# Another word order for the steady part of a fused convolution and SwiGLU kernel, and a list of its own for the second pair

## The chip, the cores and the metric

The kernel runs on one core of a Trainium2 chip. The metric is the device time of one execution in microseconds (us), the median over the runs shown. A core has a matrix engine (TensorE, PE; its weight loads are listed apart as PEld), VectorE (DVE), ScalarE (ACT), GpSimd (POOL), and SyncE (SP), on whose queue nearly all DMAs of this kernel are issued, each queue strictly in program order.

## What is computed

```python
# x: (8, 4096, 192), weight: (8 heads, 7 taps)
w = softmax(weight)                                    # over the taps
y[b, s, h, :] = sum_k w[h, k] * x_pad[b, s + k, h, :]  # causal, 24 channels a head
# y as (32768, 192); w_gate, w_val: (192, 1536), w_out: (1536, 192)
xn = y / sqrt(mean(y * y) + 1e-6) * rms_g
g, val = xn @ w_gate, xn @ w_val
out = (silu(g) * val) @ w_out                          # float32
```

## The kernel before

The 32768 tokens are cut into 32 pairs (p = 0 to 31) of 1024 tokens, each two blocks of 512. Pair 0 runs in its own prologue, pair 1 in plain float32 products (word list PLAIN for TensorE, FIRST for the rest). Pairs 2 to 31 are alike and make up most of the time.

**Gate products.** A pair's projections onto gate and value columns use a Strassen-like scheme: sums of blocks of the tokens times sums of blocks of the weights, 68 products a pair (names such as P1.0, Q3.5, Ab.3: kind, then column group j = 0 to 5). One product (`product`, L910) is 6 matmuls: the tokens were split into three parts whose products add up to float32 accuracy, and each part runs as two matmuls of 64 rows side by side. Its weights come from a ring of 10 slots in SBUF. There are 48 weight pieces a pair; when a piece's last product is recorded, the load of a new one into its slot (L790) is put on SP's queue, where it waits for that product. Products accumulate in PSUM banks (j, a) to (j, d); PSUM holds four such double banks, and `open` takes the one that is free, first come, first served.

**Between the products.** For each j: `f1` (ScalarE) copies bank a into b, `f3` (ScalarE) copies c into an SBUF tile, `f4` and `f5` (VectorE, L981) add that tile and b into c and into a new bank d. `g` (ScalarE, L987) takes the silu of the gate half of a bank, `m` (VectorE, L994) multiplies it with the value half into an SBUF tile, and with that the bank is free. So a chain Ag, Vm stands behind the last product of every bank: for (3,a) the last product is Ea.3, then come Aga.3 and Vma.3.

**o-steps.** The projection onto w_out is again Strassen-like: seven forms o1 to o7 for six j, 42 steps of 6 matmuls with tiles of 128 by 32 (`step`, L937), into accumulators X, Y, Z. The first step of form 1 opens X. Their inputs are the m tiles and sums of them (`h1` to `h4`, L964, on VectorE or GpSimd). `c1`, `c2`, `s7` copy accumulators, `C22` and `C21` (L1011) add them, `T11` to `T22` (L952) transpose results, `st` stores them.

**Work ahead for the next pairs.** `cv0` to `cv6` are the seven taps of the convolution (VectorE, L445; cv0 on ScalarE), `sq`, `red`, `pow`, `bc`, `mul` the norm, `pl.0` to `pl.7` put the result away to DRAM, `ft.0` to `ft.5` fetch it back turned (L646; for i = 1 and 3 nothing is issued), `x1` to `x4` (L832) form sums of token blocks, and `n`, `l`, `d` (L675, L818, L820) split the tokens into three parts, `ld.0` to `ld.7` load x.

**The order.** It is written by hand as words, one list for each pair (ORDER for all from 2 on), and recorded in that order; every engine runs its own words as they stand. The first letter is the engine (V VectorE, G GpSimd, A ScalarE, S SP's queue), then the action and its index; `+` and `-` shift the pair (`+` the next, `++` the one after, `-` the one before). `p3` records the next 3 entries of the pair's TensorE order LINE, `p3-` 3 of the pair before. LINE thus fixes TensorE's own order, ORDER where the rest stands against it. A tile framework adds the waits. In FIRST and for pair 1, a `+` word that was already done is skipped when it comes again.

Before, LINE has all 68 products and then all 42 o-steps. ORDER takes 2 products of a pair, then the last 6 steps of the pair before, then 66 products and 36 steps.

Of the kernel before, what the change touches and what calls it, by code (L numbers as in the profile page):

```python
# [20 lines left out]
def kernel(  # L21
# [36 lines left out]
    PAIRS = B * NB  # L58
# [15 lines left out]
    )  # L74
    PLAIN = (
        "a0 b0 c0 d0 o1.0 a1 b1 c1 d1 o1.1 a2 b2 c2 d2 o1.2 a3 b3 c3 d3 o1.3 a4 b4 c4 d4 o1.4",
        "a5 b5 c5 d5",
    )
    ORDER = (
# [14 lines left out]
    )  # L94
    FIRST = (
# [14 lines left out]
    )  # L110
    LINE = (
# [7 lines left out]
    )  # L119

    cst = ctx.enter_context(tc.tile_pool(name="cst", bufs=1))
# [8 lines left out]
    x_sb = {}  # L130
# [4 lines left out]
    def queue(eng):  # L135
        return nc.scalar if eng == "A" else nc.sync
# [8 lines left out]
    def load_head(p, b, t0, h, eng="S"):  # L145

        t = x_sb[p]

        def get(dst, tb, h, dims, r):
            row = x[b, t0 + tb * TB + r - HALO, h * GS :]  # L150
            src = bass.AP(
                tensor=row.tensor, offset=row.offset, ap=[dims, [D, TB + HALO - r], [1, GS]]
            )
            queue(eng).dma_start(out=dst, in_=src)

        first = int(t0 == 0)
        if first and h == 0:
            queue(eng).dma_start(out=t[0:H, 0:HALO, :], in_=zeros)
            get(t[0:H, HALO:, :], 0, 0, [GS, H], HALO)
        get(t[first * H + h :: H], first, h, [TB * D, P // H - first], 0)  # L160

    def load_part(p, h, eng):

        if h == 0:
            x_sb[p] = xs.tile([P, TB + HALO, GS], F32, name="xh")
        load_head(p, p // NB, (p % NB) * PT, h, eng)

# [203 lines left out]
    def convert_in(u):  # L371

        t = raw.pop(("in", u))
        dst = wf[:, :, u * NF : (u + 1) * NF, :].rearrange("p k f n -> p k (f n)")
        step = P if u == 0 else NF * P
        parts = [slice(i, i + step) for i in range(0, NF * P, step)]
        return [
            convert(t[:, :, c, :], exp_i[:, :, c], mf_i[:, :, c], dst[:, :, c], rg_sb, u < 2)
            for c in parts
        ]  # L380
# [5 lines left out]
    scr = {}  # L386
# [405 lines left out]
    def ring_start():  # L792
        ring[0] = spc.tile([P, NSLOT, KP * P], F32, name="ring")
        for slot in range(NSLOT):
            ring_load(slot)
# [40 lines left out]
    class Pair:  # L836
        def __init__(self, p):
            self.p = p
            self.bk, self.o_sb, self.sg = {}, {}, {}
            self.open_half, self.turned = {}, [0, 0]  # L840
            self.line = self.products()

        def hv(self, j, c):
# [74 lines left out]
        def step(self, form, k):  # L918
            b = ACC[form]
            if form in (1, 7) and b not in self.bk:  # L920
                full4.discard(self.open(b, False))
            fresh = form in (1, 7) and k == 0
            src = hs[:, k, :] if form == 5 else self.hv(k, LEFT[form])
            right = RIGHT[form][:, HOME[k]]
            self.tiles(b, [right[:, m] for m in range(NM)], src, fresh)
# [122 lines left out]
        tap(p, k, eng)  # L1048

    def put_away(p, h, eng):  # L1050
        if h == 0:
            scr[p] = dram.tile([D, PT], F32, name="xd")
        to = scr[p][:].rearrange("(h a) (b t) -> h b a t", a=GS, t=TB)
        queue(eng).dma_start(out=to[h], in_=yn[p][h::H])

    def ahead(eng, name, p):

        act, *at = name.split(".")
        i = int(at[0]) if at else 0
        if act[0] == "x":  # L1060
            x_sum(int(act[1]), eng, p)
        elif act in ("n", "l", "d"):
            split(act, i, eng, p)
        elif act == "ft":
            fetch(p, i, eng)
        elif act == "pl":
            put_away(p, i, eng)
        elif act == "ld":
            load_part(p, i, eng)
        elif act[0:2] == "cv":  # L1070
            tap_of(p, int(act[2]), eng)
        else:
            {"sq": square, "red": reduce, "pow": factor, "bc": spread, "mul": scale}[act](p)
# [124 lines left out]
    p, sl, v = plain(first_hts)  # L1198
# [46 lines left out]
    def run(words, w):  # L1245
        for word in words:
            p = w + word.count("+") - word.count("-")
            if word[0] == "p":
                for _ in range(int(word[1:].rstrip("+-"))):
                    if p in pairs:  # L1250
                        next(pairs[p].line)
            elif word == "W":
                next(ready)()
            elif word == "R":
                ring_start()
            else:
                eng, name = word[0], word[1:].rstrip("+-")
                act = name.split(".")[0]
                if act in own_acts:
                    if own_acts[act] <= p < PAIRS and (name, p) not in ahead_done:  # L1260
                        ahead(eng, name, p)
                        if w == 1:
                            ahead_done.add((name, p))
                elif p in pairs:
                    pairs[p].do(eng, name)

    run([w for row in FIRST for w in row.split()], 1)
    for w in range(2, PAIRS + 1):
        run([w for row in ORDER for w in row.split()], w)
# [1 line left out]
_INS = ['x', 'weight', 'moe_w_gate', 'moe_w_val', 'moe_w_out', 'moe_rms_g']  # L1271
# [26 lines left out]
```

## Time and profile before

| | us |
|---|---|
| median of 3 runs (2474.97 to 2477.09) | 2475.02 |
| span of the profiled execution | 2476.6 |
| the slowest of the runs | 2477.09 |

The profile is of one execution of its own. In its views PE's pieces of work are given with start, length, engine, tile, line and count. The chain that ended last is followed back from the last instruction, at each step to what released it. In the waits, a line names who waited, who released it, the total in us, how often, and the longest. In a row with windows, after the length stand the busy times of PE, PEld, DVE, ACT and POOL with counts, then the granted clock, the DMA share and GB/s. A row of a timeline ends with the engine's idle time before it and what ended it.

### The profile page before, as it was taken

To read this page: it belongs to the slowest core of one execution; us is meant where nothing else is said; L and a number is where in the kernel's file an instruction comes from. 1 tells how busy PE (TensorE), PEld (TensorE's weight loads), DVE (VectorE), ACT (ScalarE), POOL (GpSimd) and SP (SyncE) were. 2 spreads that over 40 slices of the span, in tenths; PEclk is the share of its full clock that TensorE was granted. 3 is DMA by queue.
4 is the path that set the end of the run, shared out by engine and by line. 5 is a ranking of instruction groups with operands and counts; after the bars stand their busy time and mean duration, and the time that the engine had idled before them with its cause. 6 is when DMAs were issued, how large, how long until landed. Compare 5 with 4: busy or idle time off the path is not lost.

```text
span 2476.6 us, 69229 instructions
## 1 busy us (share of the span) xinstructions
PE 2454.1 (99%) x29152; PEld 1896.0 (77%) x29152; DVE 2020.8 (82%) x2526; ACT 1018.0 (41%) x1435; POOL 836.2 (34%) x624
## 2 busy tenths in 40 slices
PE   8999999999999999999999999999999999999999
PEld 5546777877777877777787778777777877778777
DVE  8687888888888888888888887888888888888864
ACT  6443344434344334344334444343444343443332
POOL 0541333333333333334233434333433333333322
PEclk9999999999999999999999999999999999999999
DMA  7363677666687666786666777666776666876653
GB/s 151 60 205 107 171 200 194 190 161 175 173 205 185 189 162 173 176 211 178 177 167 171 191 193 191 173 167 172 199 198 187 160 172 172 205 185 192 159 162 94
DMA packets 716392, 430.55 MB, mean 174 GB/s; under 512 B 510330, under 2 KB 702386, under 8 KB 716082
## 3 DMA queue, kind: packets, MB, share of 16 engines
q1 hardware_dynamic: 712336, 425.21, 66.4%
q8 instruction: 230, 3.77, 0.7%
q10 hardware_dynamic: 3746, 0.92, 0.2%
q14 instruction: 80, 0.66, 0.1%
HBM read 366.96 MB, written 58.98 MB: 172 GB/s over the span
## 4 chain that ended last, share of the span: by engine, by line
PE 92%; DVE 4%; DMA 2%; issue 1%; ACT 1%; POOL 0%; SPq 0%; DVEq 0%; POOLq 0%; ACTq 0%
PE ps L910 54%; PE ps L937 35%; PE ps L882 2%; DMA xb<-xd 1%; DMA ring<-wd 1%; DVE y L445 0%; DVE ht L1109 0%; PE ps L408 0%; DVE ht L994 0%; DVE ps L981 0%; PE ps L528 0%; DVE part L345 0%; DVE part L330 0%; DVE ht L964 0%; ACT part L675 0%
## 5 line engine op out<-in xcount | busy, mean ns | idle before, releaser
L910 PE MATMUL ps<-part,ring 64*128 64x512 f32 x12240 | 1419.9, 389 | 3.4 <-DMA ring<-wd 2.3
L910 PEld LDWEIGHTS ps<-part,ring 64*128 64x128 f32 x12240 | 1151.3, 184 | 258.4 <-DVE ps L981 12.0
L987 ACT ACTIVATE tt<-ps 128x512 f32<-128x512 f32 x744 | 439.3, 599 | 714.5 <-PE ps L910 661.2
L994 DVE TENSOR_TENSOR ht<-ps,tt 128x512 f32<-128x512 f32 x744 | 497.7, 686 | 254.8 <-ACT tt L987 252.3
L937 PE MATMUL ps<-ht,wo_sb 128*32 128x384 f32 (+2 forms) x7272 | 468.3, 380 | 1.9 <-DVE tt L1011 1.1
L964 POOL TENSOR_TENSOR ht<-ht 128x512 f32<-128x512 f32 x180 | 273.6, 1527 | 541.6 <-PE ps L937 534.1
L937 PE MATMUL ps<-ht,x 128*32 128x384 f32 (+2 forms) x6696 | 440.3, 380 | 2.9 <-DVE ht L964 2.9
L937 PEld LDWEIGHTS ps<-ht,wo_sb 128*32 128x32 f32 x7272 | 325.0, 110 | 115.8 <-issue 14.8
L937 PEld LDWEIGHTS ps<-ht,x 128*32 128x32 f32 x6696 | 300.3, 110 | 93.0 <-DVE ht L964 3.1
L981 DVE TENSOR_TENSOR ps<-ps,tt 128x1024 f32<-128x1024 f32 x240 | 295.8, 1233 | 52.6 <-ACT tt L675 23.0
L445 DVE SCALAR_TENSOR_TENSOR y<-xh,tp,y 128x1536 f32<-128x1536 f32 x186 | 336.5, 1809 | 0.2
L675 ACT COPY ps<-ps 128x1024 f32<-128x1024 f32 (+1 forms) x151 | 134.6, 892 | 402.8 <-PE ps L910 326.1
L675 ACT COPY tt<-ps 128x384 f32<-128x384 f32 (+1 forms) x182 | 151.7, 834 | 225.0 <-PE ps L937 161.0
L964 POOL TENSOR_TENSOR hs<-ht 128x512 f32<-128x512 f32 x120 | 155.4, 1295 | 262.0 <-DVE ht L994 262.0
L474 POOL TENSOR_SCALAR r<-r 128x8 f32<-128x8 f32 x31 | 6.2, 199 | 509.8 <-DVE r L469 509.7
L937 PE MATMUL ps<-hs,x 128*32 128x128 f32 (+2 forms) x2232 | 161.2, 379 | 0.0
L964 DVE TENSOR_TENSOR ht<-ht 128x512 f32<-128x512 f32 x192 | 132.7, 705 | 21.3 <-PE ps L937 18.3
L937 PEld LDWEIGHTS ps<-hs,x 128*32 128x32 f32 x2232 | 106.8, 110 | 29.7
L964 DVE TENSOR_TENSOR ht<-hs,ht 128x512 f32<-128x512 f32 x156 | 112.2, 766 | 11.0 <-PE ps L937 10.2
L820 DVE SCALAR_TENSOR_TENSOR part<-part,xb 128x1024 fp32r<-128x1024 f32 x87 | 120.1, 1380 | 0.0
L818 POOL TENSOR_TENSOR part<-xb,part 128x1024 fp32r<-128x1024 f32 x29 | 69.6, 2401 | 122.3 <-PE ps L910 86.1
L495 POOL TENSOR_TENSOR xh<-y,s 128x1536 f32<-128x1536 f32 x30 | 89.9, 2997 | 15.3 <-DVE s L487 7.7
(132 smaller groups left out, 1421.1 us busy)
## 6 DMA issues: line engine op xcount, KB each, us to landing
ring<-wd SPq DMA_DIRECT2D x1440, 192.0 KB
xb<-xd SPq DMA_DIRECT2D x60, 512.0 KB
xd<-xh SPq DMA_DIRECT2D x240, 96.0 KB
xh<-in_x_dram SPq DMA_DIRECT2D x192, 105.0 KB
xb<-xd SPq DMA_DIRECT2D x60, 256.0 KB
out_dram<-o_sb SPq DMA_DIRECT2D x126, 96.0 KB
out_dram<-o_sb SPq DMA_DIRECT2D x62, 128.0 KB
wd<-part SPq DMA_DIRECT2D x5, 1152.0 KB
```

The source lines that it names most:

```text
L445: nc.vector.scalar_tensor_tensor(out=y, in0=xk, scalar=w, in1=y, op0=ALU.mult, op1=ALU.add)
L495: e.tensor_tensor(out=yn[p].rearrange("p a t -> p t a"), in0=y, in1=ss[:].rearrange("p (t o) -> p t o", o=1).to_broadcast([P, TB, GS]), op ...
L675: nc.scalar.copy(out=dst, in_=src)
L818: e.tensor_tensor(out=split_of(g, 1).bitcast(F32R), in0=src, in1=high, op=ALU.subtract)
L820: nc.vector.scalar_tensor_tensor(out=split_of(g, 2).bitcast(F32R), in0=high, scalar=1.0 + SPLIT, in1=src, op0=ALU.mult, op1=ALU.subtract,)
L882: nc.tensor.matmul(out=self.both(j, c)[:, h, :], lhsT=wf[HALF[h], k, 2 * HOME[j] + f, :], rhs=rb[HALF[h], k, g, :], start=(k == 0), stop=( ...
L910: nc.tensor.matmul(out=self.both(j, c)[:, h, :], lhsT=left[HALF[h]], rhs=right[HALF[h]], start=(first and q == 0), stop=True, skip_group_c ...
L937: nc.tensor.matmul(out=self.acc(b)[i * Q : (i + 1) * Q, at : at + n], lhsT=left, rhs=cols, start=fresh, stop=True, skip_group_check=True, ...
L964: engine[eng].tensor_tensor(out=dst, in0=a, in1=b, op=op)
L981: nc.vector.tensor_tensor(out=self.both(j, c), in0=self.both(j, "b"), in1=s5, op=ALU.add)
L987: nc.scalar.activation(out=tt[:, t, :], in_=self.both(j, c)[:, 0, :], func=AF.Silu)
L994: nc.vector.tensor_tensor(out=self.hv(j, "abcd".index(c)), in0=self.both(j, c)[:, 1, :], in1=tt[:, t, :], op=ALU.mult,)
```

## The change

LINE and ORDER are replaced, the second pair (p = 2) gets a list SECOND of its own, PLAIN now spells out the old order of the steps for pair 1, and the end of FIRST is altered. Small helpers are loosened so that parts may come in any order.

TensorE's order. Before:

```
P5.0 P1.0 P2.0 Q1.0 P6.0 Ab.1 Bb.1 Eb.1 P7.0 Q2.0 Aa.1 P3.0 Ea.1 Ba.1 P4.0 Q3.0 Q4.0
P1.2 ...
... Eb.3
Q4.4 Q3.4 P4.4 P1.5 Aa.3 Ba.3 P5.5 P6.5 Ea.3 P2.5 Q1.5 P7.5 Q2.5 P3.5 Q3.5 Q4.5 P4.5
o1.0 o7.0 o1.4 o1.2 ... o5.5 o2.4 o3.3 o3.1 o3.0 o3.5 o3.2 o3.4
```

After:

```
P1.0 P5.0 Q1.0 P6.0 P2.0 Ab.1 Eb.1 Bb.1 P7.0 Q2.0 P3.0 Aa.1 Ea.1 P4.0 Q3.0 Ba.1 Q4.0
P1.2 ...
Ec.1 Q4.2 Ad.1 Q3.2 P1.4 Ed.1 Bd.1 P5.4 Q1.4 P6.4 P2.4 Ab.3 Bb.3 P7.4 Eb.3 P3.4 Q2.4
P4.4 Q3.4 Q4.4 P1.5 Aa.3 Ba.3 P5.5 Ea.3 P2.5 P6.5 o1.0 o1.2 Q1.5 P7.5 P3.5 Q2.5 o1.3
o1.1 P4.5 Q4.5 Q3.5 o1.4 o1.5 ... o4.5 o4.2 o3.1 o3.4 o3.5 o3.3 o3.0 o3.2
```

The words, cut to the places of interest:

```diff
     ORDER = (
-        "p2 Vl.2 VC22- VT11- p3- Vd.4 VT22- VT21- Vcv3+ p3- Af1.0 Af3.0 VT12- p4 Aga.0 Vcv4+",
...
-        "Spl.5+ Spl.6+ Spl.7+ Vmc.1 p3 Agd.1 Vmd.1 p2 Af3.4 p1 Vf4.4 p4 Aga.4 Sft.0+ Sft.1+",
...
-        "Sst1.0- Sst1.2- Sst1.3- Vh1.4 Vh3.4 Vh3.0 Vf4.5 An.0+ Aga.3 p3 Vma.3 p2 Gl.0+ Gh3.3",
-        "Gx3+ Vf5.5 Aga.5 Agc.5 Vma.5 Vmc.5 p3 Vx1+ Agd.5 Agb.5 An.1+ Vx2+ p11 Vmd.5 Vh2.4",
...
-        "Vcv2++ Vd.1+ p3 Gh4.1 VC21 Gh4.4 Gh4.2",
+        "Gh4.2- p3- p1 p1- VC21- VT21- p1- Af1.0 p1- p1 Vcv2+ p1 Vcv5+ p1 Af3.0 Vcv4+ VT12-",
+        "p1 Aga.0 p2 Vf4.0 p1 Sst0.2- Agb.1 p3 Vcv3+ Vma.0 p1 Agc.0 Vmb.1 Vf5.0 p1 Vmc.0 p2",
...
+        "Vmc.1 Agb.2 p1 Vmd.2 p1 Spl.5+ p1 Spl.4+ Vmb.2 Af1.4 Spl.1+ Agd.1 p3 Af3.4 p1 Vmd.1",
+        "Aga.4 Vf4.4 p5 Sft.0+ Vma.4 Vh3.0 Agb.3 p1 Vf5.4 p1 Vmb.3 Agc.4 Spl.6+ p1 Sst0.1-",
+        "Vmc.4 Agb.4 Vmb.4 p1 Sft.5+ Agd.4 Vmd.4 p2 Af1.5 Sft.2+ p2 Sld.1++ Gh1.2 p3 Sft.4+",
+        "An.0+ Sld.3++ Aga.3 Vh1.4 Vh3.4 Af3.5 Sld.6++ Vma.3 p2 Vf4.5 p2 Aga.5 p1 Gh1.1 Vma.5",
+        "Vf5.5 p1 Sst1.0- p2 Gh3.1 Vd.0+ Agc.5 Vx1+ Sld.7++ p1 Gh1.3 Sld.0++ Gh3.2 p1 Vx2+",
...
+        "p1 Vcv6++ VT11 VC22 Gh4.4 p2 VT22",
     )
+    SECOND = (
+        "VC22- VT11- p1 p3- VT22- Af1.0 VT21- p1 p1- Vcv2+ p1- p1 p1- Vcv5+ p1 Af3.0 VT12-",
+        "Vcv4+ p1 Aga.0 p2 Vf4.0 p1 Agb.1 p3 Sst0.4- Vcv3+ Sst0.2- Vma.0 Sst1.4- p1 Agc.0",
...
     FIRST = (
...
-        "p9 Vh4.2 Acv0++ p2 Vh4.1 p1 Vcv1++ p1 VC21 p1 Vh4.4 Vcv2++",
+        "Vh4.0 R p1 As7 p1 Sld.5++ p2 Sld.6++ p1 Sld.7++ p2 Ac2 p1 Vh4.3 p9 Vh4.2 Acv0++ p2",
+        "Vh4.1 p2 VC21 p1 Vh4.4 Vl.2+ Vd.4+ Vcv6++",
...
     def load_part(p, h, eng):
 
-        if h == 0:
+        if p not in x_sb:
...
-            fresh = form in (1, 7) and k == 0
+            fresh = (b not in self.begun) and form in (1, 7)
+            self.begun.add(b)
...
     def put_away(p, h, eng):
-        if h == 0:
+        if p not in scr:
...
     run([w for row in FIRST for w in row.split()], 1)
-    for w in range(2, PAIRS + 1):
+    run([w for row in SECOND for w in row.split()], 2)
+    for w in range(3, PAIRS + 1):
         run([w for row in ORDER for w in row.split()], w)
```

Every VectorE, GpSimd and ScalarE word of ORDER stays on its engine. The taps now come as cv0 and cv6 two pairs ahead, then cv2, cv5, cv4, cv3, cv1. `l.2`, `d.4`, `C22`, `T11` and `T22` move from the start of the next pair to the end of their own, `C21` the other way. The second pair's list differs from ORDER in its start and in the places of the stores.

In the changed file `product` is at L932, `step` at L960, `g` at L1010, `m` at L1017, `f4` and `f5` at L1004.

More of the change, by code (lines that the diff above doesn't have):

```diff
@@ L76 @@
         "a0 b0 c0 d0 o1.0 a1 b1 c1 d1 o1.1 a2 b2 c2 d2 o1.2 a3 b3 c3 d3 o1.3 a4 b4 c4 d4 o1.4",
-        "a5 b5 c5 d5",
[3 rows of a table added]
     )
     ORDER = (
[14 rows of a table removed]
[15 rows of a table added]
+    )
+    SECOND = (
[15 rows of a table added]
     )
@@ L840, in __init__ @@
             self.open_half, self.turned = {}, [0, 0]
+            self.begun = set()
+            self.at = {}
             self.line = self.products()
```

59 rows, old and new, of tables (FIRST, LINE, ORDER, PLAIN) are left out of this document.

## The prediction

> **What bounds the kernel now.** I read the page first: busy shares, granted clock, and the chain that ended last.
>
> ```profile
> span 2476.6 us, 69229 instructions
> PE 2454.1 (99%) x29152; PEld 1896.0 (77%) x29152; DVE 2020.8 (82%) x2526; ACT 1018.0 (41%) x1435; POOL 836.2 (34%) x624
> ...
> PEclk9999999999999999999999999999999999999999
> ...
> PE 92%; DVE 4%; DMA 2%; issue 1%; ACT 1%; POOL 0%; SPq 0%; DVEq 0%; POOLq 0%; ACTq 0%
> ```
>
> TensorE (PE) is the chain nearly everywhere, and at full clock. A busy share of 99% hides short gaps, because matmul ends are modelled, so I next read the chain over one steady pair, where it is all PE:
>
> ```profile
> 1193.96 1.59 PE ps L910 x12
> 1195.55 4.04 PE ps L937 x48
> 1199.59 45.59 PE ps L910 x396
> 1245.18 23.54 PE ps L937 x288
> 1268.72 1.59 PE ps L910 x12
> ```
>
> L910 is gate products (6 matmuls each, tiles of 64 by 128), L937 is o-steps (128 by 32). A pair is 68 products and 42 steps, and here it is cut into four stretches: 2 products, the last 6 steps of the pair before, 66 products, 36 steps. It repeats after 1268.72 - 1193.96 = 74.76 us. Over that period the other engines have room:
>
> ```profile
> 1199.59:1274.35 74.76, 74.76 (x914) 58.62 (x914) 62.18 (x76) 30.86 (x42) 26.33 (x19) 1.00 0.69 182
> ```
>
> VectorE (DVE, third figure after the length) is busy 62.18 us of 74.76, GpSimd 26.33. So what VectorE or GpSimd save counts only where PE waits for them. Those places are seen on the weight loads (PEld), first in time order, then summed over 300 to 2400 us:
>
> ```profile
> 1209.83 16.91 PEld L910 LDWEIGHTS ps<-part,ring 64*128 64x128 f32 x150 [0.23 <-DVE ht L994]
> 1226.89 15.53 PEld L910 LDWEIGHTS ps<-part,ring 64*128 64x128 f32 x138 [0.15 <-ACT ps L675]
> 1242.82 1.93 PEld L910 LDWEIGHTS ps<-part,ring 64*128 64x128 f32 x18 [0.39 <-DVE ps L981]
> ```
> ```profile
> PEld ps L910 <- DVE ps L981: 11.2, 27, 0.6
> ...
> PEld ps L910 <- DVE ht L994: 6.4, 28, 0.2
> ...
> PEld ps L910 <- DMA ring<-wd: 4.5, 6, 1.4
> PEld ps L910 <- ACT ps L675: 4.2, 27, 0.2
> ```
>
> Three short waits a pair, each at the same product, and rarely one for a ring load. I now take the pair apart. A product is (1226.89 - 1209.83) / 25 = 0.682 us. The stretch of 2 products lasts 1.59, which is 0.225 over 2 x 0.682. The stretches of 36 and 6 steps give a step of (23.54 - 4.04) / 30 = 0.65 us, and 0.14 over. So one round trip from products to steps and back costs 0.225 + 0.14 = 0.365 us beside the work. The long stretch is 45.59 = 66 x 0.682 + 0.225 + 0.355, and the 0.355 are the three waits. Check: 68 x 0.682 + 42 x 0.65 + 2 x 0.365 + 0.355 = 74.76, the period seen. The same stretch of the first and the last whole period stands at
>
> ```profile
> 295.25 1.58 PE ps L910 x12
> ...
> 2392.05 1.58 PE ps L910 x12
> ```
>
> which is 74.89 for each of 28 pairs: all the longer stalls together are 28 x 0.13 = 3.5 us.
>
> **The change part by part.** All engines keep the same instructions in the same numbers; only order changes, so the 68 products and 42 steps keep their price.
>
> **More switches.** In the new ORDER and LINE a steady pair runs, in PE order: 3 old steps, P1.0, 3 old steps, 60 products up to P6.5, o1.0 o1.2, 4 products, o1.3 o1.1, 3 products, 32 steps that join the next pair's first 3. That is 4 round trips for 2: +2 x 0.365 = +0.73 us a pair. Bounds: no row shows a stretch as short as one product or two steps; if the cost lay in the length it would be near 0, if each switch costs what both lengths above show it is 0.73. I take 0.73, since a stretch of 2 products and one of 66, of 6 and of 36 steps, fit one figure.
>
> The Trainium skill, "TensorEngine Tiling (Array Packing)", Key Properties, says "Mode switching requires drain": a change of tiling mode empties the engine, whatever follows. By that rule the short stretches pay in full, as I took it; by length alone the sum would be 21 us less.
>
> **The three old waits go.** The 0.39 before Q3.5 is for Vf5.5 (L981), which reads bank b that Q3.5 adds to. The new line puts o1.3 o1.1, P4.5 and Q4.5 between Vf5.5 and Q3.5, 2.7 us where there was nothing. The other two, at P1.2 and P6.4, stand after other products now (Q4.0 behind Ba.1, Q1.4 ahead of P6.4). I take all of 0.355 back; bounds 0 and 0.355.
>
> **A new wait at o1.0.** It opens accumulator X in the first bank that comes free: that of (3,a), which is free once Vma.3 (L994) has read it. Ahead of Vma.3 stands Aga.3 on ScalarE, and the new order, like the old, has An.0+ in front of Aga.3; An.0+ reads the tokens that Sft.0+ fetches. The old trace shows this very chain where it ended last:
>
> ```profile
> 1007.55 7.44 DMA xb<-xd
> 1014.99 0.02 issue
> 1015.02 1.05 ACT part L675
> 1016.06 0.51 ACT tt L987
> ...
> 1016.60 0.70 DVE ht L994
> ...
> 1017.39 1.25 DVE ps L981
> ...
> 1018.68 2.33 PE ps L910 x18
> ```
>
> From the fetch's landing to the end of Vma.3 it takes 1.05 + 0.51 + 0.70 and some 0.15 of hops, 2.4 us. Before, Vf5.5 (1.25) followed and Q3.5 waited for it, 14 products (9.55 us) behind the fetch: a landing up to 5.8 us was free. Now Sft.0+ stands behind product 50 on SyncE's (SP's) queue, behind the ring loads that those products release, and o1.0 stands behind product 61: 11 products, 7.5 us, less 2.4 leaves 5.1 us for the landing. How long that is:
>
> ```profile
> 708.47 0.42 SPq L646 DMA_DIRECT2D xb<-xd  x1
> ```
> ```profile
> 713.90 1.05 ACT L675 CAST part<-xb 128x1024 fp32r<-128x1024 f32 x1
> ```
> ```profile
> ACT part L675 <- DMA xb<-xd: 2.6, 5, 1.4
> ```
>
> One fetch had landed within 713.90 - 708.47 = 5.43 us with no wait; 5 of 28 made ScalarE wait, the longest 7.44. The landing is bounded by about 4.5 (no row shows it; my estimate, a us under the shortest) and 7.44, so the wait by 0 and 2.3. I take a mean landing of 5.6: 0.5 us. Even with the tokens there, Ea.3, Aga.3, Vma.3 and o1.0 are a tight chain: 0.51 + 0.70 and hops against two products, 1.36 us, so with some 0.1 for restarting I put the wait at 0.6 us a pair. Behind o1.0 the whole PE queue stands. The old long stalls of this chain, within the 3.5 us above, end in it. Sft.0+ also needs put-aways 0 to 5; the last of them stands 9 products (6.1 us) ahead of it, where it was 10, so I add nothing for them.
>
> **The second pair.** The chain at its start in the old trace:
>
> ```profile
> 216.91 1.81 DVE y L445
> 218.72 0.47 DVE tt L1011
> 219.19 0.60 DVE ht L964
> 219.79 1.73 DVE y L445
> 221.52 0.48 DVE tt L1011
> ...
> 222.04 4.11 PE ps L937 x48
> ```
> ```profile
> 222.46 1.18 DVE L820 SCALAR_TENSOR_TENSOR part<-part,tt 128x1024 fp32r<-128x1024 f32 x1
> ```
>
> Steps o3 of pair 1 wait for VC22 (L1011 at 221.52). In the new FIRST the first tap (1.81) is gone, but Vd.4+ (1.18) and Vcv6++ (1.73) stand between Vh4.4 and VC22. Vh4.4 still ends near 219.7, as it follows PE's last steps (about 218.9), so VC22 ends near 219.6 + 1.1 + 1.73 + 0.48 = 222.9: 0.9 later. SECOND has one product ahead of the steps, not two, so 0.68 of work no longer covers it: +1.6. SECOND has 5 round trips, +1.1; VectorE, 0.9 late and with four taps of 1.8 to do, has products 9 to 14 wait for L981 and L994, +1 (bounds 0 and 2); with 0.6 - 0.355 as in other pairs, +4 in all.
>
> **Moved at no cost.** Stores, put-aways and x loads take other places on SP's queue; their cover is the depth of the ring (10 slots, at about 48 pieces a pair some 10 us ahead), and where it is too thin the price is a wait for a ring load, of which the old trace has six, 4.5 us in all; I add none. Taps, x-sums and splits on VectorE have 12 us of slack a pair. Dropped Sft.1+ and Sft.3+ issue nothing. PLAIN spells out the old step order for pair 1.
>
> **VectorE beside GpSimd.** What the order separates is real:
>
> ```profile
> 1246.29 0.69 DVE L832 TENSOR_TENSOR tt<-tt,xb 128x512 f32<-128x512 f32 x1
> ...
> 1247.50 1.38 DVE L964 TENSOR_TENSOR ht<-hs,ht 128x512 f32<-128x512 f32 x1
> ```
> ```profile
> 1247.06 1.28 POOL L832 TENSOR_TENSOR tt<-xb,tt 128x512 f32<-128x512 f32 x1 [1.98 <-DVE tt L832]
> ```
>
> The same shape takes 0.69 alone and 1.38 begun under GpSimd's operation. But this happens among o-steps, with PE on the chain; I count 0. The Trainium skill, "SBUF — State Buffer", SBUF: two separate sides, calls the shared port pair an exclusive lock that such a VectorE operation and a GpSimd one hold for a whole instruction; the trace agrees, and the rule speaks for the change only as the first rival has it.
>
> **Sum**, against the profiled execution (2476.6, 1.6 over the median of the runs, 2475.02): 29 steady pairs x (0.73 - 0.355 + 0.6) = +28; second pair +4; the old long stalls -3.5: about +28.5 to 2505, that is 2503 in terms of the runs.
>
> **The rivals.** *VectorE's late work was PE's limit, and the order frees it:* waits of 0.355 go in 30 pairs (-10.7), long stalls (-3.5), and the short stretches switch for nothing: 2462, or 2461 in terms of the runs. For it: the waits name VectorE and ScalarE. Against: two stretch lengths each give the same switch cost. It decides if a switch costs under 0.18. 6%. *Nothing shows:* a switch costs half in the short stretches, the landing is always under 5 us and the second pair pays 2, with the long stalls gone: 29 x (0.365 - 0.355) + 2 - 3.5 = -1, 2474; it needs everything else to go well. 8%. *Switches cost, no wait at o1.0:* 29 x 0.375 + 4 - 3.5 = +11, 2486. 17%. *Fetch lands late,* as the stores and ring loads now close to it share the DMA engines: 7 us at the mean makes the wait 2: 29 x 2.4 + 4 = +74, 2549. 9%. *Forecast,* 2492 to 2525: 60%.
>
> **How the numbers follow.** Range: from the rival without the wait (2485, half of it) to a mean landing of 6 us or a second pair at twice its price (2530). Chances, with 0.2% (5 us) as what a measurement here can tell from no change: faster 0.06, same 0.08, slower 0.86.
>
> **What would show it.** In the chain over a steady pair: eight stretches for four, a period near 75.7, each short stretch some 0.2 over its work; PEld of L960 (L937 before) waiting for DVE ht L1017 once a pair; no wait for L1004 before Q3.5; the first o3 steps of pair 1 later against pair 2's first product; VectorE's busy time less by some tens of us with no gain from it. A period of 74.4 or less would prove the forecast wrong, and short stretches with no excess would show why.

## The result, and the profile after

| | median, us | runs |
|---|---|---|
| kernel before | 2474.99 | 4, 2474.35 to 2477.09 |
| changed kernel | 2531.34 | 4, 2523.77 to 2535.28 |

The ratio is 1.0222, with a 95% interval from 1.0205 to 1.0239: 2.2% slower, 56 us where 28 were forecast. The profiled execution of the changed kernel is the fastest of the four (2523.77); its span is 45.4 us longer than that of the kernel before.

The page of the changed kernel, with the rows that answer to those shown of before:

```profile
span 2522.0 us, 69476 instructions
PE 2474.9 (98%) x29152; PEld 1898.8 (75%) x29152; DVE 2007.3 (80%) x2526; ACT 1027.8 (41%) x1435; POOL 794.7 (32%) x624
...
PE 84%; DMA 6%; DVE 4%; ACT 2%; SPq 1%; POOL 1%; issue 1%; DVEq 0%; ACTq 0%; POOLq 0%
```

VectorE is busy 13.5 us less and GpSimd 41.5 us less than before, and the time did not fall with them: PE's share of the chain fell from 92% to 84%, and that of DMAs rose from 2% to 6%. The chain that ended last, over one steady pair (start, length, engine, tile, line, count; L932 are products, L960 steps):

```profile
1219.93 0.91 PE ps L932 x6
1220.83 2.09 PE ps L960 x24
1222.92 33.57 PE ps L932 x294
...
1256.51 0.32 SPq L810
...
1256.93 5.33 DMA xb<-xd
...
1262.34 1.05 ACT part L695
1263.39 0.57 ACT tt L1010
...
1263.99 0.70 DVE ht L1017
...
1264.73 1.51 PE ps L960 x16
1266.24 2.95 PE ps L932 x24
1269.19 1.44 PE ps L960 x16
1270.63 2.26 PE ps L932 x18
1272.89 22.89 PE ps L960 x280
1295.78 0.91 PE ps L932 x6
```

The eight stretches are there, each with its excess. Once a pair the chain leaves PE: a ring load's issue on SP's queue, the fetch, the cast, the silu, Vma.3, then o1.0, exactly the chain that the prediction built. The shortest period in the trace is 75.13 us, and 68 x 0.682 + 42 x 0.65 + 4 x 0.365 = 75.14: round trips at their forecast price, old waits gone. The mean period over 28 pairs is 76.30. What stands over the shortest is in two places, by the starts of PE's stretches: the stretch of 60 products is 0.77 over its shortest (the wait at o1.0), and the stretch of 35 steps, called the tail below, 0.33, in nine pairs of 28 and up to 3.67. The prediction has no term for the second. The waits of PE and of its weight loads between 300 and 2400 us (total, how often, longest):

```profile
PE ps L960 <- DVE ht L1017: 14.9, 18, 2.0
PE ps L960 <- POOL ht L987: 4.8, 7, 2.2
```
```profile
PEld ps L960 <- DVE ht L1017: 26.9, 27, 2.4
...
PEld ps L932 <- DVE ps L1004: 0.6, 2, 0.3
```

The wait before Q3.5 (L1004) is gone, the wait at o1.0 has taken its place, and steps wait for a sum on GpSimd.

### The profile page after: what moved, and what is told of

Same layout as the page of the kernel before. It is cut to its first block, busy times and chain, and to the rows that moved or that the text cites. A ratio compares the mean times of both kernels' runs of the same rounds, so it can differ in the third digit from the quotient of the medians.

```text
span 2522.0 us, 69476 instructions
## 1 busy us (share of the span) xinstructions
PE 2474.9 (98%) x29152; PEld 1898.8 (75%) x29152; DVE 2007.3 (80%) x2526; ACT 1027.8 (41%) x1435; POOL 794.7 (32%) x624
## 4 chain that ended last, share of the span: by engine, by line
PE 84%; DMA 6%; DVE 4%; ACT 2%; SPq 1%; POOL 1%; issue 1%; DVEq 0%; ACTq 0%; POOLq 0%
PE ps L932 49%; PE ps L960 34%; DMA xb<-xd 5%; PE ps L904 1%; DVE ht L1017 1%; ACT part L695 1%; POOL ht L987 1%; ACT tt L1010 1%; SPq L258 0%; DVE y L465 0%; DVE ht L987 0%; SPq L810 0%; DVE ht L1132 0%; SPq L174 0%; DVE part L840 0%
## 5 line engine op out<-in xcount | busy, mean ns | idle before, releaser
L932 PE MATMUL ps<-part,ring 64*128 64x512 f32 x12240 | 1429.8, 390 | 2.2 <-DMA ring<-wd 1.8
L932 PEld LDWEIGHTS ps<-part,ring 64*128 64x128 f32 x12240 | 1158.6, 185 | 246.0 <-issue 22.0
L1010 ACT ACTIVATE tt<-ps 128x512 f32<-128x512 f32 x744 | 444.8, 598 | 788.3 <-PE ps L932 646.7
L1017 DVE TENSOR_TENSOR ht<-ps,tt 128x512 f32<-128x512 f32 x744 | 503.9, 687 | 327.5 <-ACT tt L1010 321.0
L960 PE MATMUL ps<-ht,wo_sb 128*32 128x384 f32 (+2 forms) x7272 | 472.4, 383 | 27.0 <-DVE ht L1017 17.3
L960 PEld LDWEIGHTS ps<-ht,wo_sb 128*32 128x32 f32 x7272 | 314.7, 110 | 170.5 <-issue 43.2
L960 PE MATMUL ps<-ht,x 128*32 128x384 f32 (+2 forms) x6696 | 429.8, 381 | 3.8 <-DVE ht L987 3.8
L987 POOL TENSOR_TENSOR ht<-ht 128x512 f32<-128x512 f32 x180 | 240.5, 1343 | 519.5 <-PE ps L960 428.7
L960 PEld LDWEIGHTS ps<-ht,x 128*32 128x32 f32 x6696 | 303.8, 111 | 91.7 <-DVE ht L987 4.6
L465 DVE SCALAR_TENSOR_TENSOR y<-xh,tp,y 128x1536 f32<-128x1536 f32 x186 | 338.8, 1821 | 10.9 <-ACT y L461 8.7
L1004 DVE TENSOR_TENSOR ps<-ps,tt 128x1024 f32<-128x1024 f32 x240 | 295.5, 1231 | 49.8 <-PE ps L932 28.2
L960 PE MATMUL ps<-hs,x 128*32 128x128 f32 (+2 forms) x2232 | 147.5, 379 | 0.0
L960 PEld LDWEIGHTS ps<-hs,x 128*32 128x32 f32 x2232 | 98.5, 110 | 31.2
L695 ACT CAST part<-xb 128x1024 fp32r<-128x1024 f32 x87 | 90.9, 1045 | 45.1 <-DMA xb<-xd 39.3
L840 DVE SCALAR_TENSOR_TENSOR part<-part,xb 128x1024 fp32r<-128x1024 f32 x87 | 105.9, 1218 | 0.0
L461 ACT ACTIVATE y<-xh,tp 128x1536 f32<-128x1536 f32 x29 | 45.8, 1579 | 114.0 <-DMA out_dram<-o_sb 68.6
```

Of the source, the lines that this page charges most:

```text
L461: nc.scalar.mul(y, xk, w)
L465: nc.vector.scalar_tensor_tensor(out=y, in0=xk, scalar=w, in1=y, op0=ALU.mult, op1=ALU.add)
L695: nc.scalar.copy(out=dst, in_=src)
L840: nc.vector.scalar_tensor_tensor(out=split_of(g, 2).bitcast(F32R), in0=high, scalar=1.0 + SPLIT, in1=src, op0=ALU.mult, op1=ALU.subtract,)
L932: nc.tensor.matmul(out=self.both(j, c)[:, h, :], lhsT=left[HALF[h]], rhs=right[HALF[h]], start=(first and q == 0), stop=True, skip_group_c ...
L960: nc.tensor.matmul(out=self.acc(b)[i * Q : (i + 1) * Q, at : at + n], lhsT=left, rhs=cols, start=fresh, stop=True, skip_group_check=True, ...
```

## The experiments

All times are medians, beside runs of the kernel before on the same chip. They were taken in four sets (x1 to x4, x5 to x8, x9 to x11, x12), so from one set to another the ratios compare better than the medians. In the stretches of PE, "over" means the mean above the shortest such stretch of the changed kernel. Words of ORDER were moved in SECOND in the same way.

**x1, the cast out of the chain.**

```diff
-Sft.4+ An.0+ Sld.3++ Aga.3 Vh1.4 Vh3.4 Af3.5 Sld.6++ Vma.3 p2 Vf4.5
+Sft.4+ Sld.3++ Aga.3 Vh1.4 Vh3.4 Af3.5 Sld.6++ Vma.3 An.0+ p2 Vf4.5
```

> The changed kernel with one word moved in ORDER and SECOND: the cast of the fetched tokens (An.0+) behind the read that frees bank (3,a) (Vma.3), no longer ahead of Aga.3 on ScalarE. In the changed kernel's trace a steady pair has 1.17 us over its work and its four round trips (76.30 mean against 68 x 0.682 + 42 x 0.65 + 4 x 0.365 = 75.13). Theory A, the late landing of the fetch causes most of it at o1.0: the wait for DVE ht L1017 falls to about 0.1 a pair, the mean period to about 75.45, the time by 0.85 x 29 = 25 us to about 2506. Rival, ScalarE and VectorE are late at bank (3,a) whatever the cast does (0.57 + 0.70 and hops behind Ea.3 against two products): half a microsecond a pair stays, the gain is under 12 us. Rival, the cast done later is missed by what reads the parts next (the l and d words, the next pair's first products): the wait turns up there and the time stays within 5 us of 2531.

Measured 2523.65 us (2517.87 to 2530.73), ratio 1.0197 [1.0179, 1.0214]. The wait at o1.0 fell from 0.77 to 0.25, but the time by only 3 to 8 us (from x5's 2527 or the first 2531) where 25 were forecast, which the spread of the runs hardly tells from nothing. Its chain over the next stretch shows why:

```profile
2174.19 0.61 ACT tt L1010
...
2174.82 0.70 DVE ht L1017
...
2175.57 1.51 PE ps L960 x16
...
2180.67 2.01 DVE part L840
...
2184.00 1.21 DVE ht L1017 x2
...
2185.26 17.86 PE ps L960 x216
```

PE now comes to o7.4 before its bank is free: Vmc.5 and Vmd.5 (L1017) stand behind d.0 (L840) and the token sums (L852) on VectorE. The 35 steps never take less than 23.19, 0.30 over 22.89, in all pairs, and on the mean they are 0.78 over for 0.33 in the changed kernel. So 0.45 of the 0.52 came back there. Both the landing and VectorE's queue behind it hold that place, and what came out is what the first rival said: half a microsecond a pair stays (0.25 and 0.30), and the gain is under 12 us.

**x2, the same move in the kernel before.**

```diff
-Vf4.5 An.0+ Aga.3 p3 Vma.3
+Vf4.5 Aga.3 An.0+ p3 Vma.3
```

> The kernel before with the same word move in ORDER: An.0+ behind Aga.3 on ScalarE. There the chain from the fetch's landing runs An.0, Aga.3, Vma.3, Vf5.5, Q3.5, and the wait for L981 costs 0.6 at most a pair (11.2 us over 27 pairs), with long stalls of 3.5 us in all. If that chain makes these waits, it becomes about 1 us shorter (1.05 for the cast) and they shrink to 0.1 a pair or less: 30 x 0.25 + 3.5 = about 11 us less, 2464. If the wait before Q3.5 is made by VectorE's own queue (Vf4.5, Vma.3, Vf5.5 back to back behind other work), it stays: gain under 3 us.

Measured 2474.61, before 2474.75, ratio 0.9997 [0.9988, 1.0006]. The wait for L981 stayed, 11.0 us in 28 waits, and in all of them Vf5.5 itself was released by a product on PE. In the old order that wait is not the fetch's: Vf5.5 follows P7.5 with only two products to cover it. The theory that the fetch's chain makes it fell.

**x3, one more round trip in the kernel before.**

```diff
-p2 Vl.2 VC22- VT11- p3- Vd.4 VT22- VT21- Vcv3+ p3- Af1.0
+p1 Vl.2 VC22- VT11- p3- Vd.4 VT22- VT21- Vcv3+ p1 p3- Af1.0
```

> The kernel before with one more round trip between products and steps a pair, and nothing else moved but two words' places: one product, three old steps, one product, three old steps, 66 products, 36 steps. If each switch costs a fixed price whatever the length of the stretch, as the prediction took it: 0.365 x 30 = 11 us more, 2486, the period 75.1, the stretch of one product 0.91 and that of three steps 2.09. If the cost lies in something that a short stretch doesn't have: 0 to 3 us more.

Measured 2491.31 (2490.43 to 2492.19), before 2474.75: +16.6, ratio 1.0065 [1.0052, 1.0078]. The chain around the split (L910 products, L937 steps, C22 on L1011):

```profile
2104.96 0.56 DVE tt L1011
...
2105.57 2.16 PE ps L937 x24
2107.72 0.89 PE ps L910 x6
2108.62 2.09 PE ps L937 x24
2110.71 45.52 PE ps L910 x396
```

One product alone takes 0.89 and three steps 2.09, which is 0.21 and 0.14 over their work. The prediction had 0.225 after two products and 0.14 after 6 and 36 steps, so a switch costs the same after one product and after three steps: 0.35 a pair, 10.5 us. C22 takes 4 us more, as one product no longer covers it (the stretch in front of its steps is 0.14 longer in most pairs than the other of one product). No row shows the remaining 2 us. The Trainium skill, "TensorEngine Tiling (Array Packing)", Key Properties, says that a change of tiling mode drains the engine; the trace agrees, with 0.35 a round trip here.

**x4, another order of the last six steps.**

```diff
-o3.1 o3.4 o3.5 o3.3 o3.0 o3.2
+o3.5 o3.3 o3.0 o3.1 o3.4 o3.2
```

> The changed kernel with its last six steps in another order: o3.5 o3.3 o3.0 o3.1 o3.4 o3.2 in place of o3.1 o3.4 o3.5 o3.3 o3.0 o3.2, so that the step that reads GpSimd's sum Gh4.1 comes three steps (1.95 us) later. In the changed kernel's trace PE waits for POOL ht L987 seven times, 4.8 us in all, and PE's chain shows stretches of the tail up to 3.7 us over their work in 12 of 28 pairs, 0.33 a pair on the mean. If GpSimd's sum, stretched from 1.29 to 2 to 4 us beside VectorE's two-input work, is what is late: the waits go and the time falls by about 0.33 x 29 = 10 us to about 2521. If VectorE's own sums (h4.5, h4.3) are as late, they take its place, as they are wanted three steps earlier: 0 to 4 us less, or more than before.

Measured 2521.35 (2520.49 to 2526.93), ratio 1.0191 [1.0177, 1.0205]. The waits of PE in it:

```profile
PE ps L960 <- DVE tt L1034: 8.3, 6, 2.1
```

GpSimd is no longer named, C22 is (L1034). The time is the forecast one, but not by the forecast way, which is luck: the stretch of 35 steps still is 0.26 over, so the tail gave back only 0.07 a pair, 2 us. GpSimd was only the last of several that were late together.

**x5, the changed kernel again**, without an edit.

> The changed kernel once more, beside the others and the kernel before. Its four runs spread from 2523.77 to 2535.28 and the profiled one was the fastest, while the kernel before spreads over 3 us. If the spread comes from when the fetched tokens land (they stand in the chain once a pair), a second profile shows another mean wait at o1.0 and the same 75.13 us of work and switches a pair. If it comes from elsewhere, the other parts of the pair change. Median expected between 2524 and 2534.

Measured 2527.03 (2524.14 to 2535.49), ratio 1.0214 [1.0198, 1.0229]. A second profile gives the same account: 0.78 at o1.0, 0.39 in the tail, shortest period 75.13. The medians 2531.34 and 2527.03 are the baselines for the other changes of this kernel; differences of some 4 us from them say nothing. What makes its runs spread over 11 us wasn't settled: both profiled executions were the fastest of their four, so no trace shows a longer one.

**x6, C22 ahead of the tap.**

```diff
-Vh4.3 p2 Vh4.0 p1 Vcv6++ VT11 VC22 Gh4.4
+Vh4.3 p2 Vh4.0 p1 VC22 Vcv6++ VT11 Gh4.4
```

with the o3 order of x4.

> The o3 order of x4_o3_order, and in ORDER and SECOND the word VC22 ahead of the tap Vcv6++ (1.73) on VectorE. In x4 the wait for GpSimd was gone, but the steps o3 waited for DVE tt L1034 instead, 8.3 us over 6 times, so that the stretch of 35 steps still had 0.28 us a pair over its 22.89. If VectorE's order in the tail is what is left (the tap stands in front of C22), these waits go: the stretch comes to 22.9 to 23.0 on the mean, 0.2 x 29 = 6 to 8 us less than x4's 2521, about 2514. If C22 is late for what it reads (the last form 5 step and the copy), the waits stay and the time is x4's.

Measured 2515.84 (2514.07 to 2517.15), ratio 1.0160 [1.0147, 1.0174], as expected: the tail is 0.03 over. But the 60 products are now 0.90 over, and some of them wait for the transposes behind the tap (DVE o_sb L975, 8.0 us in 8 waits). So the tap itself is late; C22 only stood behind it.

**x7, the second pair.**

```diff
 FIRST
-Vh4.1 p2 VC21 p1 Vh4.4 Vl.2+ Vd.4+ Vcv6++
+Vh4.1 p2 VC21 p1 Vh4.4
 SECOND
-VC22- VT11- p1 p3- VT22- Af1.0 VT21- p1 p1- Vcv2+
+VC22- VT11- p1 p3- Vl.2 Vd.4 VT22- Af1.0 VT21- Vcv6+ p1 p1- Vcv2+
```

> The changed kernel with the end of FIRST as short as the old one: Vl.2+, Vd.4+ and Vcv6++ leave it and stand in SECOND behind the three old steps (Vl.2 and Vd.4 ahead of VT22, Vcv6+ behind VT21). In the changed kernel, from the second pair's first product to the third pair's takes 84.52 us, 6.6 more than before when the shift of three steps is taken off. If VectorE's order in front of C22 makes the wait at the first o3 steps (1.6 us in the prediction), that stretch becomes 1.5 to 2.5 us shorter, 82 to 83. If VectorE simply has too much to do there, the three words are late behind the steps instead, the products wait for L1004 or the casts, and it stays at 84 to 85.

Measured 2520.28 (2514.82 to 2526.25), ratio 1.0181 [1.0165, 1.0197]. The chain at the start of the second pair, in the changed kernel and in this one:

```profile
219.29 1.22 DVE part L840
220.51 1.73 DVE y L465
222.24 0.48 DVE tt L1034
...
222.76 3.63 PE ps L960 x24
```
```profile
219.01 0.47 DVE tt L1034
```

C22 comes 3.2 us earlier, and the second pair lasts 300.03 - 218.21 = 81.8 us for 303.09 - 218.57 = 84.5. Of the 6.6 us over the old second pair (84.5 less 75.94 before, less three steps that are moved work, 1.95) 2.7 went; 3.9 stay, with VectorE's taps still in the chain. The forecast was met, but part of the 2.7 is not the wait itself. In the changed kernel PE stands still for 3.23 us in front of these three steps, and then they take 3.63 us where three steps otherwise take 2.09: the profile grants TensorE only half its clock (0.50 from 224 to 226) for about 3.4 us, which costs 1.7. Here the pause is 0.37 and the clock stays at 1.00. No row shows the rest of the 7 to 11 us between the medians; the tail of this profile is worse, 0.59 over.

**x8, more VectorE work in the kernel before.**

```diff
-Vh1.5 Vh3.5
+Vh1.5 Vh1.5 Vh3.5
```

> The kernel before with one VectorE operation more a pair among the o-steps: the sum h1.5 is formed twice, with the same result, 0.7 to 1.4 us. If VectorE has room there, as its 62 us of 74.76 suggest and as the prediction took it when it counted the separation from GpSimd at 0, the time stays within 2 us of 2475. If VectorE is what holds TensorE there by its order (sums that steps wait for), 0.2 to 0.7 us a pair shows: 6 to 20 us more, and then what the change saves on VectorE could have been worth as much.

Measured 2477.21, before 2475.62, ratio 1.0006 [0.9998, 1.0015]. Its page:

```profile
PE 2455.4 (99%) x29152; PEld 1887.4 (76%) x29152; DVE 2046.7 (83%) x2556; ACT 1018.0 (41%) x1435; POOL 854.6 (34%) x624
```

25.9 us more of busy VectorE cost 1.6 us, which the interval doesn't tell from 0. There is room among the o-steps, so what the separation saves there was worth next to nothing in the old order.

**x9, o1.0 one product later.**

```diff
-Ea.3 P2.5 P6.5 o1.0 o1.2 Q1.5 P7.5 P3.5 Q2.5 o1.3
+Ea.3 P2.5 P6.5 Q1.5 o1.0 o1.2 P7.5 P3.5 Q2.5 o1.3
```

> The changed kernel with two entries of LINE swapped: product Q1.5 ahead of o1.0 o1.2 in place of behind them, so that o1.0 is wanted 0.68 us later; all words stay. In the changed kernel's two profiles the stretch of 60 products waits 0.73 and 0.78 us a pair over its shortest, 41.16. If the wait at o1.0 is itself what costs, nearly all of it goes, 0.6 x 29 = 17 us less than the changed kernel's 2527 to 2531, about 2512. If VectorE's chain from bank (3,a) on (Vma.3, f4.5, Vma.5, f5.5, the splits, Vmc.5) is what holds TensorE, the wait moves to P7.5 (DVE ps L1004) or to o7.4 (DVE ht L1017) and the time stays within 5 us.

Measured 2522.83 (2513.38 to 2535.41), ratio 1.0188 [1.0164, 1.0213]. The wait at o1.0 fell to 0.28 as the first theory has it, but the gain was lost elsewhere, though not at P7.5 or o7.4: the tail rose from 0.33 to 0.90, with five periods of 78.7 to 80.3. Neither theory had that. Behind PE's pause in four of these five tails the granted clock is 0.50 for about 3.4 us, as in x7. What made more such tails here than in the changed kernel wasn't settled.

**x10, x6, x7 and x9 together.**

> The changed kernel with the swap of x9_o1_one_later, the o3 order and C22 ahead of the tap of x6_c22_ahead, and the short end of FIRST of x7_second_pair. If the four causes add up (o1.0 17, the tail 12, the second pair 3), 2529 - 32 = 2497, the steady period 75.2 to 75.4. What then is left over the kernel before, about 22, is the price of the two more round trips, 0.73 x 29 = 21, less the old waits of 0.355 a pair that are gone, 10, and the rest of the second pair and of the chance stalls. If the causes hide behind one another, it stays above 2506.

Measured 2508.39 (2499.16 to 2514.88), ratio 1.0130 [1.0111, 1.0149]: they don't add up. A part of its chain over one pair (L174 x load, L1066 store, L461 the first tap cv0, L465 a tap, L975 transposes):

```profile
1199.14 0.88 SPq L174
...
1200.06 0.68 SPq L1066
...
1200.79 0.88 SPq L174
...
1201.71 2.55 DMA out_dram<-o_sb
1204.26 1.58 ACT y L461
...
1209.87 1.82 DVE y L465
...
1215.31 0.65 DVE o_sb L975 x2
...
1216.00 39.08 PE ps L932 x342
```

Here the chain runs back from a product over transposes, taps and the first tap to loads and stores being issued one by one on SP's queue. That turned the question to the moved DMAs. The same in the changed kernel, in the tail of one pair:

```profile
902.78 0.88 SPq L174 DMA_DIRECT2D xh<-in_x_dram  x1
...
907.00 1.58 ACT L461 ACTIVATE y<-xh,tp 128x1536 f32<-128x1536 f32 x1 [6.34 <-DMA xh<-in_x_dram]
908.03 4.01 POOL L987 TENSOR_TENSOR ht<-ht 128x512 f32<-128x512 f32 x2 [13.98 <-PE ps L960]
908.62 2.30 DVE L465 SCALAR_TENSOR_TENSOR y<-xh,tp,y 128x1536 f32<-128x1536 f32 x1 [2.03 <-ACT y L461]
...
911.41 0.51 DVE L1034 TENSOR_TENSOR tt<-ps,tt 128x384 f32<-128x384 f32 x1
```
```profile
912.06 3.44 PE L960 MATMUL ps<-ht,wo_sb 128*32 128x384 f32 x36 [2.18 <-POOL ht L987]
```
```profile
914.00:916.00 2.00, 2.00 (x20) 1.08 (x12) 1.96 (x2) 0.00 (x0) 0.00 (x0) 0.50 0.00 0
```

The last x load for the pair after next is issued at 902.78, cv0 starts at 907.00, VectorE stands still for 2.03 us, and then the tap runs just when GpSimd forms its two sums: 4.01 us for two that take 1.29 each alone. The Trainium skill, "SBUF — State Buffer", SBUF: two separate sides, has these two engines hold one port pair in turn; the trace agrees, with 4.01 us for 2.6 and a tap of 2.30 for 1.82. o3 waits for all of it: PE stands still for 2.18 us, and the three steps behind the pause take 3.44 us at half the clock (0.50 in the last row, the figure behind the five engines).

**x11, a version of the kernel before with one product moved.**

```diff
-Ad.1 Bd.1 P1.4 Ed.1 P5.4
+Ad.1 P1.4 Bd.1 Ed.1 P5.4
```

> The kernel before with P1.4 one product earlier in LINE (P1.4 Bd.1 Ed.1 in place of Bd.1 P1.4 Ed.1), as the changed LINE has one more product between P1.4 and P6.4 too. The wait for ACT ps L675 at P6.4, 4.2 us over 27 pairs, is a copy of 1.0 us that starts when P1.4 ends, against two products. If one product more covers it and a bank is free for P1.4 that early: 4 us less, 2471. If P1.4 then waits for its bank instead: 0, or some us more.

Measured 2474.12, before 2475.39, ratio 0.9990 [0.9981, 0.9998]. The waits of the weight loads name ACT ps L675 no more; of the 4.2 us 1.3 came through. It has the lowest median of the study, but the interval nearly reaches 1.

**x12, the x loads early.**

```diff
-Gh1.3 Sld.0++ Gh3.2 ... Sld.4++ ... Sld.5++ ... Sld.2++ As7
+Gh1.3 Sld.0++ Sld.4++ Sld.5++ Sld.2++ Gh3.2 ... As7
```

> The changed kernel with three words of SP's queue moved in ORDER and SECOND: the x loads ld.4, ld.5 and ld.2 for the pair after next directly behind ld.0, among the last products, where the kernel before has all eight, in place of among the o-steps. In the changed kernel's trace the first tap cv0 on ScalarE waits for DMAs (68.6 us in 18 waits named by out_dram<-o_sb; in the pair at 902.78 the last x load is issued, at 907.00 the tap starts behind DMA xh<-in_x_dram, then VectorE has 2.03 us idle, and tap, GpSimd's sum (4.01 us for two) and C22 are late for o3 at 912.06). The kernel before has no such wait. If the moved x loads make the tail wait, against the prediction's step that moved DMAs cost nothing: ScalarE's waits for these DMAs fall below 10 us, VectorE's for the tap too, the stretch of 35 steps comes to 22.9 to 23.0 on the mean, 0.35 x 29 = 10 us less, about 2518. If VectorE's order beside GpSimd makes it whatever the tap does: the stretch stays at 23.2 to 23.3 and the time within 4 us.

Measured 2511.80 (2509.09 to 2514.77), before 2476.30, ratio 1.0147 [1.0134, 1.0161]: 15 to 20 us less than the changed kernel by three words on SP's queue; the interval doesn't touch those of the changed kernel (from 1.0198 on). Waits of the first tap in the kernel before, and of the first tap and of VectorE for it in the changed kernel:

```profile
ACT y L441 <- DMA ring<-wd: 0.4, 1, 0.4
```
```profile
ACT y L461 <- DMA out_dram<-o_sb: 68.6, 18, 5.5
...
ACT y L461 <- DMA xh<-in_x_dram: 37.5, 9, 6.3
```
```profile
DVE y L465 <- ACT y L461: 7.9, 7, 2.0
```

and with the loads early:

```profile
ACT y L461 <- DMA xh<-in_x_dram: 13.6, 12, 2.3
...
ACT y L461 <- DMA ring<-wd: 5.0, 4, 1.9
```

106 us of waits became 19, VectorE waits for cv0 no more, the tail is 0.09 over, and no period is longer than 76.62 (79.32 before that edit). That the store was named as releaser in 18 waits was the profile's inference: the stores kept their places, and these waits went with the loads. The mean period fell from 76.30 to 75.81; 0.24 of that is the tail and 0.18 the wait at o1.0, which is 0.59 a pair now. Why the second fell isn't shown.

The tails of the other profiles say the same. In x1, x4, x5, x7, x9 and the changed kernel 17 of them are over by 2.3 us or more, and all 17 stand in the one pair of four that loads the first tokens of a sequence, which issues one more x load (L178, 0.73 us) on SP's queue. With the loads early no such pair behind the second is over at all.

## Why the prediction was right in direction and half in size

- **Bound by PE, steps and products at their price:** right. The shortest period, 75.13, is the forecast sum without waits.
- **More switches, +0.73 a pair:** right, to 0.01; x3 shows the price in the shortest stretches.
- **The three old waits go, -0.355:** right in the changed kernel. What made the one before Q3.5 was VectorE's sum behind P7.5, not the fetch (x2).
- **A new wait at o1.0, 0.6:** right in kind; 0.77 and 0.78 in two profiles, 0.59 with the x loads early. x1 adds that VectorE's queue stands close behind it: of 0.52 taken off at o1.0, 0.45 came back in the steps from o7.4 on.
- **The second pair, +4:** 84.52 against 75.94 before, of which 3 steps (1.95) are moved work: +6.6. The place was right (C22 behind a split and a tap, x7), the size too low in three terms. PE's stretches in that pair show six round trips where five were counted, so 1.46 for 1.1. The pause at C22 grew from 1.14 to 3.23 us, 2.1 for 1.6. And the half clock behind that pause, 1.7 us, had no term.
- **VectorE beside GpSimd, 0:** right as far as x8 tells. The tail shows the two still colliding, now on PE's path.
- **Moved at no cost:** this step failed. It looked for waits on ring loads and found cover for those, but not at what reads the x loads. The new ORDER issues the last three of them among the o-steps, in the pair shown the last one 4.2 us before cv0 can start; cv0, the tap, C22 and the transposes are late in turn. x12, which moves nothing else, takes 15 us (from x5) to 20 us (from the first runs) off, of the 28 that the forecast missed. In x9 a gain elsewhere was lost in these same tails; whether x6, x7 and x9 would add up with the loads early wasn't run.
- **The clock:** the prediction took it as full, as it is in the steady part of the kernel before. In the changed kernel's profile it falls to half for about 3.4 us behind three pauses of PE (at 222.8, 912.1 and 2407.0), 1.7 us each, 5 us in all; with the loads early only the first of them is left.

The account of the profiled runs: 28 x (0.73 - 0.355 + 0.77 + 0.33) = 41.3, the second pair 6.6, the old long stalls -3.5, together 44.4 of the 45.4 measured; the 5 us of half clock are within the 45.4. The medians are 56 apart since the profiled run was the fastest. The first median, 2531.3, lies just above the stated range (up to 2530), that of x5, 2527.0, inside it. With the loads early the distance to the kernel before is 35.5 us, against a forecast of 28.

## What to carry to other kernels

- For every DMA that a new order moves, name its reader and that reader's reader, and count from the issue on the queue, not from where the word stands: a late load showed here as three different waits (GpSimd, C22, transposes). Reordering for two of them (x4, x6) moved the wait on each time and gained 11 to 15 us together; moving three loads gained 15 to 20 at once.
- Where one engine is busy for 99% of the span, a reorder gains at most the waits it names (here 0.355 a pair); each split of a stretch costs a switch at once (0.35).
- A bank that is opened by the first step of a phase puts everything that frees it, down to a fetch, in front of the whole queue.

## What the hardware showed that was not expected

- A round trip between products (64 by 128) and steps (128 by 32) costs 0.35 to 0.365 us whatever the length of the stretches, down to one product (0.68 us of work).
- SP's queue is a resource by itself: in the chain of x10 an x load takes 0.88 us to issue and a store 0.68, one after the other, and the transfers start only then.
- A pause of TensorE can cost more than its length. Between 205 and 2450 us, eight of the profiles (the changed kernel, x1, x4 to x7, x9, x12) have 26 pauses of PE over 2 us, up to 3.43. With 19 of them, among them all eleven of 2.39 us or more, the granted clock is 0.50 for about 3.4 us from around PE's restart, which costs up to 1.7 us; the seven without are of 2.09 to 2.19 us, and no pause under 2 us has it.
- GpSimd's two sums took 4.01 us beside a tap on VectorE, where two of 1.29 would be 2.6; one late load was enough to bring the two together in an order written to keep them apart.
